# Seven products for the whole second layer from the third block on, with sums and copies that may change engine

## The chip, the core and the metric

The kernel runs on one core of one Trainium2 chip. The metric is the device time of one execution in microseconds. Three runs of the kernel before took 294.63 us (median), 294.39 and 295.84 us. In the profile's rows PE is TensorE (matmuls; PEld its weight loads), DVE is VectorE, ACT ScalarE, POOL GpSimd and SP SyncE.

## The reference, cut to what matters

q, k and v are float32 of 8 batches x 8 heads x 576 positions x 64. Linear attention comes first, then one feed-forward layer over 4608 tokens.

```python
q_s = softmax(q, axis=-1)          # over the 64 of the head
k_s = softmax(k, axis=2)           # over the 576 positions
kv = np.einsum('bhsd,bhse->bhde', k_s, v)
attn = np.einsum('bhsd,bhde->bhse', q_s, kv)
x = attn.transpose(0, 2, 1, 3).reshape(4608, 512)
h = x @ w_in                       # 512 x 2048
g = np.where(h > 0, h, np.exp(np.minimum(h, 0)) - 1)
out = g @ w_out                    # 2048 x 512, float32
```

## The kernel before

Attention works on 16 units (`n`, half of a batch each): q, k and v are loaded, exponentiated on ACT (`stage1`), q is divided by its row sums (reduce and reciprocal on DVE, the product with two SBUF inputs on POOL, a part of the first units on DVE, L441), v is cast to bf16 (L418), q is transposed (`tp` on PE for the first units, later `turn` by DMA and `widen`, a cast, L491/L493), k and v are multiplied (`kv_mm`, L521), scaled (`m`, L530 and L534), and the result is applied to q (`ao_mm`, L552); `xt` copies it (L586, L589) into `XT`, a ring of three blocks.

The feed-forward layer works on nine blocks `j` of 512 tokens. In layer one each block has eight steps `g`; a step is eight 128x128x512 matmuls (`hg_mm`, L637) into a PSUM pair, and steps alternate between two pairs. `hg` then empties the pair: exp on ACT into a buffer `ESB` (L653), a second ACT instruction `relu(1 - e)` in place (L673), and two DVE instructions, here called drains (L676), that combine it with PSUM and write `GR`. PE may use the pair again, two steps later, once the second drain is done. `GR` has 24 units, one and a half blocks.

Layer two of blocks 0 and 1 is plain: `out_mm` (L698) with 512-column matmuls over all 16 tiles of the inner dimension. From block 2 on it uses a seven-product scheme: two token tiles and two halves of the 512 columns form a 2x2 problem, `pair(j, ts)`, two pairs per block, each run while the next block's steps run. The inner dimension is cut into pieces z, two tiles each, gathered in groups.

```python
GROUPS, WHOLE = ((0, 4), (4, 6), (6, 8)), 6
NSP = 6
```

Groups 0 and 1 (12 of 16 tiles) always go by seven products (`mms`, L850, 256-column matmuls). Group 2, the last four tiles, does so only in blocks 6 to 8 (`groups(j)`); in blocks 2 to 5 it goes plainly, by two calls of `std` (L863), four 512-column matmuls each. Each pair and group needs four sums over `GR` (`sums` and `late`, by `add_sum`, L798): S1 = A21 + A22 into `SB`, A21 := A11 - A21, A11 := S1 - A11, A12 := A12 - A11. All are on POOL but those of the very last `late`, which are on DVE. The weights need four combinations per group (`combos`, L769, POOL), once. The products accumulate in PSUM; `copy` (L876, ACT) takes the first, and `dve` (L871) adds the rest into `OSB`, from where SP stores the rows.

The order of every engine's instructions is written out by hand as numbers, `ORDER`, one line of numbers per engine; `Sched.add` records instructions with their dependencies, and `order` and `emit` put them out in that order, with a semaphore wait where a dependency crosses engines. An instruction's engine is fixed in the code. The model times in `Sched` set no waits; they only place some spare matmuls at the start and sort the waits.

Of the kernel before, what the change touches and what calls it, by code (L numbers as in the profile page):

```python
# [21 lines left out]
NSP = 6  # L22
# [78 lines left out]
class Op:  # L101
    __slots__ = ("eng", "dur", "emit", "deps", "key", "idx", "start", "end",
                 "dma", "sem", "val", "clock", "nbytes", "follow", "side", "late", "packet", "margin",
                 "gate", "span", "behind", "early")

    def __init__(self, eng, dur, emit, key, dma=None, nbytes=0):
        self.eng, self.dur, self.emit, self.key = eng, dur, emit, key
        self.deps = {}
        self.dma, self.nbytes = dma, nbytes
        self.start = self.end = None  # L110
        self.behind, self.early = None, 0
        self.follow, self.side, self.packet, self.margin = None, 0, 4608, 0


class Sched:
# [4 lines left out]
    LAND = 350  # L120
    SPIN_FROM, WARM = 5500.0, 11300.0
    FIRST = {"sp": 2050, "act": 2050, "gp": 2700}
    DMA_RATE = 385.0

    def __init__(self, nc):
        self.nc = nc
        self.E = {"sp": nc.sync, "act": nc.scalar, "dve": nc.vector,
                  "pe": nc.tensor, "gp": nc.gpsimd}
        self.ops = []
        self.w = {}  # L130
        self.r = {}
        self.gate = None

    def add(self, eng, dur, emit, key, R=(), W=(), X=(), dma=None, nbytes=0, after=(),
            follow=None, side=0):
        op = Op(eng, dur, emit, key, dma, nbytes)
        op.idx = len(self.ops)
        op.follow, op.side, op.late, op.gate = follow, side, False, self.gate
# [22 lines left out]
    def order(self):  # L161
        line = {e: [self.ops[int(i)] for i in ORDER[e].split()] for e in self.ENG}
        free = {e: 740.0 for e in self.ENG}
        queue = {e: 0.0 for e in self.ENG}
        seq = []
        while any(line.values()):
            before = len(seq)
            for e in self.ENG:
# [104 lines left out]
def t_f32r(n):  # L273
    return (n + 32) / 2.4
# [881 lines left out]
```

## Time and profile before

| | |
|---|---|
| runs | 294.63, 295.84, 294.39 us |
| median | 294.63 us |
| profiled execution, first to last instruction (span) | 292.2 us |
| what the median holds beyond that span | 2.4 us |
| granted TensorE clock | 1.000 over the span |

The page gives no other time of the profiled execution than its span, so what lies around it is taken as the 2.4 us up to the median. A group's row gives the line, the engine, the operation, output <- input with partitions x elements, the count, then after the bar the busy time in us and the mean ns of one, and after the second bar the idle time of the engine just before such instructions, with who ended it. A row of the chain gives start, length and count. A row of waits gives the total in us, how often, and the longest.

### The profile page before, as it was taken

How to read it: one execution, taken by the hardware profiler on the slowest of the kernel's cores; microseconds unless marked ns; L12 is line 12 of the kernel's file. 1: busy time of each engine (PE TensorE's matmuls, PEld its weight loads, DVE VectorE, ACT ScalarE, POOL GpSimd, SP SyncE). 2: the span in 40 equal slices, each digit the busy share in tenths (PEclk: the TensorE clock that was granted, in tenths of full speed). 3: DMA queues.
4: the chain of work that ended last, by engine and by line, in shares of the span. 5: the costliest groups of instructions: out<-in, count | busy, mean ns of one | idle time of the engine just before them, and what ended most of it. 6: DMA issues, size and time to landing. Idle time of an engine off the chain costs nothing.

```text
span 292.2 us, 5351 instructions
## 1 busy us (share of the span) xinstructions
PE 282.1 (97%) x2128; PEld 242.1 (83%) x2128; DVE 177.4 (61%) x326; ACT 211.3 (72%) x249; POOL 220.6 (76%) x216
## 2 busy tenths in 40 slices
PE   2899999999999999999999999999999999999994
PEld 0478887778888888888988888988989889988994
DVE  3748834787464686575656675756542667356753
ACT  4858849988998989786976779856883667665610
POOL 1992435617788999899786979799678968899880
PEclk9999999999999999999999999999999999999999
DMA  7999999799995679577919476403111010400235
GB/s 254 397 367 388 389 389 335 169 281 332 274 316 125 101 232 159 168 182 254 234 45 207 150 157 202 98 16 77 38 36 36 2 31 5 110 0 2 55 90 144
DMA packets 36472, 50.01 MB, mean 171 GB/s; under 512 B 16352, under 2 KB 18144, under 8 KB 36448
## 3 DMA queue, kind: packets, MB, share of 16 engines
q1 hardware_dynamic: 29680, 33.96, 43.5%
q0 software_dynamic: 6528, 15.47, 17.6%
q10 hardware_dynamic: 240, 0.26, 0.4%
q8 instruction: 16, 0.26, 0.4%
q14 instruction: 8, 0.07, 0.1%
HBM read 36.70 MB, written 9.44 MB: 158 GB/s over the span
## 4 chain that ended last, share of the span: by engine, by line
PE 94%; DMA 2%; POOL 2%; SPq 0%; issue 0%; DVE 0%
PE PS L637 46%; PE PS L850 28%; PE PS L698 10%; PE PS L863 5%; PE PS L552 3%; DMA KR<-in_k_dram 2%; PE PS L521 2%; POOL W L379 1%; POOL VB L418 0%; PE PS L465 0%; POOL QS L441 0%; SPq L359 0%; PE PS L564 0%; DVE OSB L871 0%
## 5 line engine op out<-in xcount | busy, mean ns | idle before, releaser
L637 PE MATMUL PS<-XT,W 128*128 128x512 f32 x576 | 142.7, 393 | 0.1
L676 DVE SCALAR_TENSOR_TENSOR GR<-PS,ESB 128x512 fp32r<-128x512 f32 (+1 forms) x124 | 87.5, 705 | 59.6 <-ACT ESB L673 55.7
L637 PEld LDWEIGHTS PS<-XT,W 128*128 128x128 f32 x576 | 105.0, 188 | 21.5 <-DMA W<-in_moe_w_in_dram 0.5
L653 ACT ACTIVATE ESB<-PS 128x1024 f32<-128x1024 f32 x72 | 73.5, 1025 | 38.4 <-PE PS L637 36.9
L673 ACT ACTIVATE ESB<-ESB 128x1024 f32<-128x1024 f32 x64 | 67.8, 1060 | 1.5
L798 POOL TENSOR_TENSOR GR<-GR 128x512 fp32r<-128x512 f32 (+1 forms) x65 | 62.7, 982 | 5.5 <-PE PS L850 4.9
L871 DVE TENSOR_TENSOR OSB<-OSB,PS 128x256 f32<-128x256 f32 x84 | 34.6, 417 | 26.9 <-PE PS L850 25.7
L850 PE MATMUL PS<-W,GR 128*128 128x256 f32 x288 | 45.5, 284 | 0.0
L850 PE MATMUL PS<-TB,GR 128*128 128x256 f32 x288 | 43.8, 283 | 0.0
L441 POOL TENSOR_TENSOR QS<-QR,RZQ 128x1152 f16<-128x1152 f32 (+1 forms) x16 | 30.2, 1886 | 17.2 <-DVE RZQ L433 16.5
L850 PEld LDWEIGHTS PS<-W,GR 128*128 128x128 f32 x288 | 40.8, 190 | 2.0
L850 PEld LDWEIGHTS PS<-TB,GR 128*128 128x128 f32 x288 | 39.9, 191 | 1.7
L798 POOL TENSOR_TENSOR SB<-GR 128x256 fp32r<-128x256 f32 (+1 forms) x31 | 30.0, 973 | 11.4 <-DVE GR L676 10.4
L698 PE MATMUL PS<-W,GR 128*128 128x512 f32 x128 | 32.4, 395 | 0.0
L798 POOL TENSOR_TENSOR GR<-SB,GR 128x256 fp32r<-128x256 f32 (+1 forms) x31 | 29.9, 978 | 2.4 <-PE PS L850 1.9
L418 POOL CAST VB<-VR 128x1152 bf16<-128x1152 f32 (+1 forms) x16 | 17.7, 1106 | 16.1 <-DMA VR<-in_v_dram 16.1
L698 PEld LDWEIGHTS PS<-W,GR 128*128 128x128 f32 x128 | 23.4, 188 | 4.7 <-DVE GR L683 0.2
L430 DVE TENSOR_REDUCE ZQ<-QR 128x18 f32<-128x1152 f32 (+2 forms) x18 | 21.8, 1209 | 6.5 <-ACT QR L428 4.9
L586 ACT ACTIVATE XT<-PS 128x512 fp32r<-128x512 f32 (+6 forms) x32 | 19.2, 603 | 6.8 <-PE PS L552 3.0
L876 ACT ACTIVATE OSB<-PS 128x256 f32<-128x256 f32 x28 | 10.4, 377 | 18.3 <-PE PS L850 9.3
L402 ACT ACTIVATE KR<-KR 128x1152 bf16<-128x1152 f32 x16 | 18.4, 1157 | 0.8 <-DMA KR<-in_k_dram 0.8
L398 ACT ACTIVATE QR<-QR 128x1152 f32<-128x1152 f32 x14 | 16.3, 1161 | 1.5 <-DMA QR<-in_q_dram 1.5
(57 smaller groups left out, 220.4 us busy)
## 6 DMA issues: line engine op xcount, KB each, us to landing
out_dram<-OSB SPq DMA_DIRECT2D x61, 128.0 KB, 2.4
QR<-in_q_dram SPq DMA_DIRECT2D x12, 576.0 KB, 5.0
KR<-in_k_dram SPq DMA_DIRECT2D x12, 576.0 KB, 6.1
VR<-in_v_dram SPq DMA_DIRECT2D x12, 576.0 KB, 5.4
W<-in_moe_w_out_dram POOLq DMA_DIRECT2D x4, 1024.0 KB, 16.6
QR<-in_q_dram POOLq DMA_DIRECT2D x4, 576.0 KB, 12.1
VR<-in_v_dram POOLq DMA_DIRECT2D x4, 576.0 KB, 13.0
KR<-in_k_dram POOLq DMA_DIRECT2D x4, 576.0 KB, 11.1
```

The lines of the kernel that those rows point to most:

```text
L402: S.add("act", t_act(1152, False), lambda e: e.activation(ek[:, :, :, :].rearrange("p h c d -> p (h c d)"), flat(k), AF.Exp), key - 2, X=[ ...
L430: S.add("dve", t_dve(m), lambda e, qp=qp, zp=zp: e.tensor_reduce(zp, qp, AX.X, ALU.add), key - 3, R=[f"qR{i}{x}" for x in xs], W=[f"ZQ{i}{ ...
L441: lambda e, qp=q[:, :, a:b, :], rz=rz, dst=qs[:, :, a:b, :]: e.tensor_tensor(dst, qp, rz, ALU.mult),
L586: S.add("act", t_act((h1 - h0) * n_, True), lambda e, dst=dst, src=src: e.activation(dst, src, AF.Copy), key, W=W, X=X)
L637: last = e.matmul(P[:, t * 512:(t + 1) * 512], self.W1[:, kc, tt * 128:(tt + 1) * 128], self.XT[:, kc, rc:rc + BLK], start=(kc == 0), stop ...
L653: S.add("act", t_act(1024, True), lambda e: e.activation(esb[:, :], self.PS[ps][:, :], AF.Exp), key, W=[f"E{i}"], X=banks)
L673: S.add("act", t_act(1024, False), lambda e: e.activation(esb[:, :], esb[:, :], AF.Relu, bias=1.0, scale=-1.0), key, X=[f"E{i}"])
L676: S.add("dve", t_dve(512 if j else 1024), lambda e, u=u: e.scalar_tensor_tensor(*(x[:, :, u, :] if j else x for x in (gt, P)), 0.0, ev[:, ...
L698: last = e.matmul(dst, self.tile(jb, jj, ts), self.W2[:, jj, c0:c1], start=(jj == 0), stop=(jj == 15))
L798: lambda e: e.tensor_tensor(dst, a, b, op), key, R=R, W=W, X=X, after=after)
L850: last = e.matmul(dst, a[i][:, y_, :], b[i][:, y_, :], start=start and i == 0 and y_ == 0, stop=stop and i == len(grps) - 1 and y_ == z - ...
L871: S.add("dve", t_dve(256), lambda e: e.tensor_tensor(dst, a, b, ALU.add), key, R=R, W=W, X=X, after=after)
```

## The change

- `NSP` becomes 8 and `groups` goes: all three groups go by seven products in every block from 2 on. `std` goes. All `combos` are made at the end of block 2, and group 2's weight combination T1 overwrites the weights' quarter B12 as in the other groups.
- `TB` and `SB` grow to eight pieces. To make room, the two `ESB` buffers lie in `TB` and serve blocks 0 and 1 only. From block 2 on exp is written into the block's own units of `GR` (seen as float32 under the name `GE`), and relu and drains work there in place.
- Copies out of PSUM (`xt`, `tp`, `out_store`, `copy` in `pair`), sums, combinations, casts of v and of the transposed q can each be given to one of two engines. The engine is the one in whose line of `ORDER` the number stands.
- `ORDER` is new for all engines. PE's is the same for its first 34 rows. The constants of the model times are simplified.

In the changed kernel's order 168 sums stand instead of 136, of them 73 on DVE (3 before) and 95 on POOL (133 before). Four of the twelve combinations are on DVE. Four of the 14 later casts of v and seven more of the casts of q are on ACT, and 12 of the copies from PSUM of 256 columns, 3 of 512 and 12 of `xt` on DVE. The diff, cut to its core:

```diff
-NSP = 6
+NSP = 8
 class Sched:
-    def add(self, eng, dur, emit, key, R=(), W=(), X=(), dma=None, nbytes=0, after=(),
-            follow=None, side=0):
+        self.home = {int(i): e for e, line in ORDER.items() for i in line.split()}
+    def add(self, eng, dur, emit, key, R=(), W=(), X=(), dma=None, nbytes=0, after=(), side=0):
+        alts = eng if isinstance(eng, dict) else {}
+        if alts:
+            eng = self.home.get(len(self.ops))
+            eng = eng if eng in alts else next(iter(alts))
+            dur = alts[eng]
...
+        self.GE = nc.alloc_sbuf_tensor_at("GE", [128, 24, 2, 256], F32, offset=nc.sbuf_base - 49152)
-        self.ESB = [a(f"ESB{i}", [128, 1024], F32) for i in range(2)]
-        self.TB2 = nc.alloc_sbuf_tensor_at("TB2", [128, 4, 2, 256], F32R, offset=rbase)
-        self.SB2 = nc.alloc_sbuf_tensor_at("SB2", [128, 2, 128], F32R, offset=rbase + 8192)
+        self.ESB = [at(f"ESB{i}", [128, 1024], F32, offset=tbase + NSP * 1024 + 4096 * i)
+                    for i in range(2)]
...
 def hg(self, j, g, ps, key, how, whole=True):
-        S.add("act", t_act(1024, True), lambda e: e.activation(esb[:, :], self.PS[ps][:, :], AF.Exp), key,
-              W=[f"E{i}"], X=banks)
+        own = gw
+        if j < 2:
+            i = self.eslot % 2
+            self.eslot += 1
+            own = [f"E{i}"]
+            ge = self.ESB[i][:, :].rearrange("p (c u t) -> p c u t", c=2, u=2) if j else self.ESB[i][:, :]
+        S.add("act", t_act(1024, True), lambda e: e.activation(ge, P, AF.Exp), key, W=own, X=banks)
...
 def add_sum(self, grp, dst, a, b, op, key, R, W, X, after):
-        self.S.add(eng, n_ * 2.4 + 60 if eng == "gp" else t_dve(n_),
+        self.S.add({"gp": n_ * 2.4 + 60, "dve": t_dve(n_)}, None,
                    lambda e: e.tensor_tensor(dst, a, b, op), key, R=R, W=W, X=X, after=after)
...
 def pair(self, j, ts, key):
-        grps = self.groups(j)
-        full = 2 in grps
+        grps, tail = (0, 1, 2), j >= WHOLE
...
         def copy(dst, src, W, bk):
-            S.add("act", t_act(256, True), lambda e: e.activation(dst, src, AF.Copy), key, W=W,
+            S.add({"act": t_act(256, True), "dve": t_dve(256)}, None, lambda e: self.copy(e, dst, src), key, W=W,
                   X=[f"b{bk}"])
...
         def second():
-            if not full:
-                std(0, 2 * NSP, 16, False)
+            pass
...
         def fourth():
-            if not full:
-                std(1, 2 * NSP, 16, False)
-            elif not end:
+            if not end:
...
                     if g == 7:
-                        self.combos(key, 0)
-                        self.combos(key, 1)
+                        for grp in range(3):
+                            self.combos(key, grp)
```

More of the change, by code (lines that the diff above doesn't have):

```diff
@@ L102 @@
     __slots__ = ("eng", "dur", "emit", "deps", "key", "idx", "start", "end",
-                 "dma", "sem", "val", "clock", "nbytes", "follow", "side", "late", "packet", "margin",
-                 "gate", "span", "behind", "early")
+                 "dma", "sem", "val", "clock", "nbytes", "side", "early", "alts")
     def __init__(self, eng, dur, emit, key, dma=None, nbytes=0):
@@ L110, in __init__ @@
         self.start = self.end = None
-        self.behind, self.early = None, 0
-        self.follow, self.side, self.packet, self.margin = None, 0, 4608, 0
+        self.side = self.early = 0
 class Sched:
@@ L163, in order @@
         free = {e: 740.0 for e in self.ENG}
-        queue = {e: 0.0 for e in self.ENG}
-        seq = []
+        queue, seq = 0.0, []
         while any(line.values()):
-            before = len(seq)
+            ready = []
             for e in self.ENG:
-                while line[e]:
+                if line[e] and all(d.end is not None for d in line[e][0].deps):
                     o = line[e][0]
-                    near = [d for d in (o.follow, o.gate, o.behind) if d is not None]
-                    if any(d.end is None for d in list(o.deps) + near):
-                        break
-                    t = max([free[e]] + [d.end + self.hop(d, o) for d in o.deps] +
-                            [d.start + (d.dur if d.eng == e else 0) for d in near[:2] if d is not o.behind])
-                    o.start, o.end = t, t + o.dur
-                    free[e] = o.end
-                    if o.dma:
-                        if o.behind is not None:
-                            queue[e] = max(queue[e], o.behind.end - self.LAND - o.behind.margin)
-                        queue[e] = max(t + self.FIRST[e], queue[e]) + o.nbytes / self.DMA_RATE
-                        o.end = queue[e] + self.LAND + o.margin
-                    seq.append(line[e].pop(0))
-            assert len(seq) > before
-        rank = {o: i for i, o in enumerate(seq)}
-        return self.fill(sorted(seq, key=lambda o: (o.start, rank[o])))
+                    ready.append((max([free[e]] + [d.end + self.hop(d, o) for d in o.deps]), e))
+            t, e = min(ready)
+            o = line[e].pop(0)
+            o.start, o.end = t, t + o.dur
+            free[e] = o.end
+            if o.dma:
+                queue = o.end = max(t + self.FIRST[e], queue) + o.nbytes / self.DMA_RATE
+            seq.append(o)
+        return self.fill(seq)
     def hop(self, d, o):
@@ L198, in fill @@
             if o.eng == "pe" and not done:
-                count = int((o.start - free - 20) / 430 if free < self.WARM else
+                count = int((o.start - free - 20) / 421 if free < self.WARM else
                             (o.start - free - 150) / 260)
@@ L412, in stage1 @@
                     dst, src = VB[:, h0:h1, :, 0:D], v[:, h0:h1, :, :]
-                if eng == "act":
-                    S.add("act", t_act(int(576 * (h1 - h0)), False), lambda e, dst=dst, src=src:
-                          e.activation(dst, src, AF.Copy), key - 50, R=[vname], W=[f"VB{vb}{x}"])
-                else:
-                    S.add(eng, 77 + 488 * (h1 - h0) if eng == "gp" else t_dve(int(576 * (h1 - h0))),
-                          lambda e, dst=dst, src=src: e.tensor_copy(dst, src), key - 50,
-                          R=[vname], W=[f"VB{vb}{x}"])
+                cost = {"act": t_act(int(576 * (h1 - h0)), False), "gp": 77 + 488 * (h1 - h0)}
+                S.add(dict(sorted(cost.items(), key=lambda x: x[0] == "act" and vconv != "pair" or x[0] == "gp" and h0 == 5)),
+                      None, lambda e, dst=dst, src=src: self.copy(e, dst, src), key - 50, R=[vname], W=[f"VB{vb}{x}"])
         if "q" not in what:
@@ L436, in stage1 @@
             for a, b, ys in cuts:
-                eng = "gp" if n in self.BYPOOL and ys == [1] or n in self.ALLPOOL else "dve"
                 m = (b - a) * 128
+                cost = {"gp": m * 2.0 + 30, "dve": t_dve(m)}
+                if n in self.BYPOOL and ys == [0]:
+                    cost = {"dve": t_dve(m), "gp": m * 2.0 + 30}
                 rz = self.RZQ[i][:, :, a:b].unsqueeze(3).broadcast_to([128, 2, b - a, D])
-                S.add(eng, m * 2.0 + 30 if eng == "gp" else t_dve(m),
+                S.add(cost, None,
                       lambda e, qp=q[:, :, a:b, :], rz=rz, dst=qs[:, :, a:b, :]: e.tensor_tensor(
@@ L470, in tp @@
             W = [f"qsT{self.alt(n)}{x}" for x in W]
-            if eng == "act":
-                S.add("act", t_act(n_, True), lambda e, dst=dst, src=src: e.activation(
-                    dst, src, AF.Copy), key, W=W, X=X, after=after)
-            else:
-                S.add("dve", t_dve(n_), lambda e, dst=dst, src=src: e.tensor_copy(dst, src),
-                      key, W=W, X=X, after=after)
+            cost = {"act": t_act(n_, True), "dve": t_dve(n_)}
+            S.add(dict(sorted(cost.items(), reverse=eng == "dve")), None,
+                  lambda e, dst=dst, src=src: self.copy(e, dst, src), key, W=W, X=X, after=after)
     def turn(self, n, key):
@@ L489, in widen @@
         src = self.QT[:, :, :].rearrange("p c t -> p (c t)")
-        if n >= LATE:
-            self.S.add("gp", 1080, lambda e: e.tensor_copy(dst, src), key, R=["QT"], W=W)
-        else:
-            self.S.add("act", t_act(1152, False), lambda e: e.activation(dst, src, AF.Copy), key,
-                       R=["QT"], W=W)
+        cost = {"act": t_act(1152, False), "gp": 1080}
+        self.S.add(dict(sorted(cost.items(), reverse=n >= LATE)), None, lambda e: self.copy(e, dst, src), key,
+                   R=["QT"], W=W)
     def side(self, ps, key, *parts):
@@ L758, in combos @@
         z0, z1 = GROUPS[grp]
-        if grp == 2:
-            early = [f"qR0{x}" for x in range(2)] + ["kR0"]
-        else:
-            early = [f"Ox{i}{x}" for i in range(4) for x in "LR"]
-        old, hi = [f"B{grp}"], grp == 2
-        for s, (dst, a, b, W, X, R) in enumerate((
-                (T3, B22, B12, [f"T1{grp}"] + early, [], self.w2(grp)),
-                (T1, B12, B11, [f"T3{grp}"] + [] if hi else [f"T3{grp}"] + self.w2(grp), [], []),
-                (T2, B22, T1, [f"T0{grp}"], [], [f"T3{grp}"]),
-                (T4, B21, T2, [f"T2{grp}"], [], [f"T0{grp}"]))):
-            S.add("gp", (z1 - z0) * 256 * 2.34 + 30, lambda e, dst=dst, a=a, b=b: e.tensor_tensor(
-                dst, a, b, ALU.subtract), key, R=R, W=W, X=X, after=S.ops[-1:] if s == 1 else S.r["qR00"][-1:] if hi and s == 0 else ())
-    def groups(self, j):
-        return (0, 1, 2) if j >= WHOLE else (0, 1)
+        early = [f"Ox{i}{x}" for i in range(z0 // 2, z1 // 2) for x in "LR"]
+        for s, (dst, a, b, W, R) in enumerate((
+                (T3, B22, B12, [f"T1{grp}", f"E{min(grp, 1)}"], self.w2(grp)),
+                (T1, B12, B11, [f"T3{grp}"] + self.w2(grp), []),
+                (T2, B22, T1, [f"T0{grp}"] + early, [f"T3{grp}"]),
+                (T4, B21, T2, [f"T2{grp}"], [f"T0{grp}"]))):
+            n_ = (z1 - z0) * 256
+            S.add({"gp": n_ * 2.34 + 30, "dve": t_dve(n_)}, None, lambda e, dst=dst, a=a, b=b: e.tensor_tensor(
+                dst, a, b, ALU.subtract), key, R=R, W=W, after=S.ops[-1:] if s == 1 else ())
     def sb(self, j, ts, grp):
@@ L805, in sums @@
             S1, N = self.sb(j, ts, grp)
-            own = [f"T1{grp}"] if grp == 2 and (j, ts) != (NBLK - 1, 1) else []
-            one = self.add_sum(grp, S1, A21, A22, ALU.add, key, h + g + own, N, [], self.summed.get(N[0], []))
+            one = self.add_sum(grp, S1, A21, A22, ALU.add, key, h + g, N, [], self.summed.get(N[0], []))
             self.third[j, ts, grp] = self.add_sum(grp, A21, A11, A21, ALU.subtract, key, m, [], h, [one])
@@ L856, in mms @@
                       R=list(names[i]) + ([f"T{wnames}{grp}"] if wnames is not None else self.w2(grp)))
-        def std(p, jj0, jj1, stop):
-            bk = (b0, b1)[p]
-            def mm(e):
-                for jj in range(jj0, jj1):
-                    last = e.matmul(self.bank(bk), self.tile(j, jj, 2 * ts + p), self.W2[:, jj, :],
-                                    start=False, stop=stop and jj == jj1 - 1, skip_group_check=True)
-                return last
-            S.add("pe", (jj1 - jj0) * t_f32r(512), mm, key, side=2, X=[f"b{bk}"],
-                  R=self.gnames(j, ts, range(jj0 // 2, jj1 // 2)) + [
-                      f"W2_{s}" for s in range(jj0 // 4, (jj1 + 3) // 4)])
         def dve(dst, a, b, R, W, X, after=()):
@@ L951, in program @@
         self.xt(1, 0, 0, -10, XT1)
-        for o in S.ops:
-            if o.eng == "pe":
-                o.late = False
         S.spare_after = [self.ident]
```

125 lines of the change are left out of this document (42 added, 83 removed), and 120 rows, old and new, of the table ORDER.

## The prediction

> **What bounds the kernel now.** I read the page's busy times first, then its chain of work that ended last.
>
> ```profile
> span 292.2 us, 5351 instructions
> PE 282.1 (97%) x2128; PEld 242.1 (83%) x2128; DVE 177.4 (61%) x326; ACT 211.3 (72%) x249; POOL 220.6 (76%) x216
> PE 94%; DMA 2%; POOL 2%; SPq 0%; issue 0%; DVE 0%
> ```
>
> PE carries 94% of the chain. The rest lies before 14 us and after the last matmul. Then I looked at the chain in order of time, here one early piece and a stretch in the fourth block:
>
> ```profile
> 54.16 2.14 PE PS L637 x8
> ...
> 102.60 0.93 PE PS L863 x4
> 103.53 1.82 PE PS L637 x8
> 105.35 0.95 PE PS L850 x8
> 106.30 1.84 PE PS L637 x8
> 108.14 1.43 PE PS L850 x12
> ```
>
> From 102 on each piece starts where the one before ends (102.60 + 0.93 = 103.53), so PE waits for nobody: only less PE work shortens the kernel, and only a new wait of PE lengthens it. The rows give my prices: 1.82/8 = 0.2275 us for a 512-column matmul, 0.93/4 = 0.23 for one in L863, 1.43/12 = 0.119 for a 256-column one. The other engines matter only where they release PE. The next rows show how far they are from that, and what their instructions cost.
>
> ```profile
> DVE GR L676 <- ACT ESB L673: 55.7, 46, 5.3
> L653 ACT ACTIVATE ESB<-PS 128x1024 f32<-128x1024 f32 x72 | 73.5, 1025 | 38.4 <-PE PS L637 36.9
> L673 ACT ACTIVATE ESB<-ESB 128x1024 f32<-128x1024 f32 x64 | 67.8, 1060 | 1.5
> L871 DVE TENSOR_TENSOR OSB<-OSB,PS 128x256 f32<-128x256 f32 x84 | 34.6, 417 | 26.9 <-PE PS L850 25.7
> L798 POOL TENSOR_TENSOR GR<-GR 128x512 fp32r<-128x512 f32 x27 | 35.0, 1299 | 4.5 <-PE PS L850 4.3
> L441 POOL TENSOR_TENSOR QS<-QR,RZQ 128x1152 f16<-128x1152 f32 x12 | 25.9, 2155 | 3.5 <-DVE RZQ L433 2.8 <-DMA QT<-QS 0.7
> L418 POOL CAST VB<-VR 128x1152 bf16<-128x1152 f32 x14 | 16.1, 1149 | 16.1 <-DMA VR<-in_v_dram 16.1
> L491 POOL CAST qsT<-QT 128x1152 fp32r<-128x1152 f16 x10 | 11.5, 1154 | 3.4 <-PE PS L552 2.3 <-PE PS L521 1.1
> L769 POOL TENSOR_TENSOR TB<-W 128x1024 fp32r<-128x1024 f32 x2 | 4.8, 2410 | 0.1
> L589 DVE CAST XT<-PS 128x512 fp32r<-128x512 f32 x2 | 1.4, 692 | 2.0 <-PE PS L564 2.0
> L589 DVE CAST XT<-PS 128x256 fp32r<-128x256 f32 x1 | 0.4, 425 | 0.6 <-PE PS L552 0.6
> ```
>
> DVE spends 55.7 us waiting for ACT before its drains (L676): this idle time is PE's cover, because DVE is nearly always ready when a bank is.
>
> **Part one: PE's work.** In blocks 2 to 5 (counted from 0), eight pairs lose two `std` calls of four 512-column matmuls each: 64 of them, 64 x 0.23 = 14.7 us (0.2275 each would give 14.6). Each pair gains seven products of two 256-column matmuls: 8 x 14 = 112, at 0.119 13.3 us. All of it is on the path. Net, with 0.1 for a last group being a little slower after a change of width (1.84 against 1.82 above): **-1.25 us**. [...]
>
> **Part two: who does the rest.** Group 2 adds four sums in each of eight pairs, 32 in all, of 256 elements. The changed order holds 168 sums and 12 weight combinations. On POOL 25 sums of 512 and 13 of 256, 3 combinations of 512 and 1 of 1024, 4 casts of v and 7 of qsT go away:
>
> ```profile
> L798 POOL TENSOR_TENSOR GR<-GR 128x256 fp32r<-128x256 f32 x38 | 28.4, 756 | 1.0 <-PE PS L850 0.6
> ```
>
> 25 x 1.30 + 13 x 0.75 + 3 x 1.30 + 2.4 + 4 x 1.15 + 7 x 1.15 = 61 us, so POOL falls from 221 to 160 us. ACT takes the 11 casts (12.7 us) and gives up 12 copies of 256, 3 of 512 and 12 of XT, some 14 us: no change. DVE takes these copies (16 us, at 0.43, 0.69 and, for XT, the same per column) and 74 more sums and combinations whose two inputs both lie in SBUF (77 against 3): 47 of 256, 29 of 512, one of 1024. Their price is in the last three sums of the old kernel, and in four products of stage one:
>
> ```profile
> L798 DVE TENSOR_TENSOR GR<-GR x3: 417/501/919, 282.4 to 284.1; 128x256 fp32r<-128x256 f32 x2, 128x512 fp32r<-128x512 f32 x1
> L441 DVE TENSOR_TENSOR QS<-QR,RZQ x4: 818/822/974, 8.3 to 37.2; 128x640 f16<-128x640 f32 x4
> 280.79 3.13 POOL L798 TENSOR_TENSOR GR<-GR 128x512 fp32r<-128x512 f32 x3
> 282.40 0.92 DVE L798 TENSOR_TENSOR GR<-GR 128x512 fp32r<-128x512 f32 x1
> 283.70 0.84 DVE L798 TENSOR_TENSOR GR<-GR 128x256 fp32r<-128x256 f32 x2 [0.38 <-PE PS L850]
> 36.47 1.06 POOL L441 TENSOR_TENSOR QS<-QR,RZQ 128x512 f16<-128x512 f32 x1
> 37.24 0.97 DVE L441 TENSOR_TENSOR QS<-QR,RZQ 128x640 f16<-128x640 f32 x1
> ```
>
> The 640-element product takes 0.82 and once 0.97. That one began at 37.24, while POOL's product ran until 36.47 + 1.06 = 37.53; it ended at 38.21, 0.68 after POOL's end. The sum of 282.40 stretched likewise behind POOL's second sum, POOL's three took 3.13 instead of 1.30 + 2 x 0.75 = 2.8, and of the two sums of 256 the one that began before POOL's end took 0.50, the other 0.42. So a sum on DVE that meets a POOL instruction waits out its rest, less about 0.15 that its own start hides (0.29 of rest cost 0.97 - 0.82 = 0.15). Unmet, a sum costs 0.42 (256) or about 0.68 (512, estimate: 0.92 less the 0.24 of its meeting).
>
> DVE's work then is 177 + 16 + 47 x 0.42 + 29 x 0.68 + 1.2 - 1.7 = 232 us (79%), before meetings. POOL is busy with such instructions for some 147 us, half of the span. Weighted by length (65 sums of 0.75, 35 of 1.30, 3 of 2.4, 12 of 2.16, 17 of about 1.15) the rest of one that is met is 0.65 us, 0.5 after the hidden part: **0.25 us for each of the 77 sums, 19 us in all**. Bounds: below, 0.15 a sum, if POOL often idles just then (it waits for DVE's sums, too); above, 0.4, where both run sums back to back. [...]
>
> **Part three: what DVE's lateness does to PE.** Mostly nothing: DVE has 60 us free. But the new order packs sums ahead of drains in one queue, and behind a late sum stand the drains, for which PE's next step on that PSUM pair waits. Take the change from block 6 to 7. Between the last product of block 5 and the product that needs `copy`'s half bank again, PE has two steps (16 x 0.2275) and 38 products' matmuls (38 x 0.119), 8.2 us. A matmul's start lies 0.28 ahead of its end, though the ends are 0.12 apart, and DVE must be done before that start; with 0.2 to 0.3 more on the way at both ends (estimate) about 7.7 is left. DVE has there, in this order, one OSB add, five drains, eight sums (six of 256, two of 512) and the copy.
>
> ```profile
> L850 PE MATMUL PS<-W,GR 128*128 128x256 f32 x288 | 45.5, 284 | 0.0
> L676 DVE SCALAR_TENSOR_TENSOR GR<-PS,ESB 128x512 fp32r<-128x512 f32 x120 | 82.6, 689 | 58.9 <-ACT ESB L673 55.0 <-PE PS L850 2.0
> ```
>
> 0.42 + 5 x 0.69 + 6 x 0.42 + 2 x 0.68 + 0.43 = 8.2, less 0.08 for each of ten that overlap the one before (0.50 + 0.42 took 0.84 above): 7.4. Room 0.3; eight sums at 0.25 cost 2.0; PE waits 1.7. In the same way I count 13.8 us of DVE work in 13.8 with six sums from block 5 to 6 (late by 1.5), and 14.6 in 15.4 with nine, POOL's combinations of 2.4 us beside them, from block 2 to 3 (late by 1.4). Together **+4.6 us**. Each is paid once, since a waiting PE lets DVE catch up. Lighter packings (3 to 4, 4 to 5, in 7) would add up to 1.7; I leave them covered. With 0.15 a sum the three give 2.2, with 0.4 and the lighter ones about 10.
>
> **Smaller edits, at nothing.** `hg` writes exp into GR and works in place, so exp waits for GR's last reader; in the new order those readers end ahead of the step's matmuls, but for the fifth step of blocks 7 and 8 (0.7 us after), whose bank has 5.2 us of PE work against a drain chain of about 4 (1.03 + 1.06 + 2 x 0.69 + hand-overs): covered. Without that cover it is 0.7 each. Start, W1 and W2 loads and first 34 rows of PE are in the same order. SP issues block 0's stores ahead of a transpose and loads; their readers come later. Eleven casts now stand ahead of exps on ACT and could wait for a load:
>
> ```profile
> 66.94 1.15 POOL L418 CAST VB<-VR 128x1152 bf16<-128x1152 f32 x1 [7.22 <-DMA VR<-in_v_dram]
> 81.17 1.15 POOL L418 CAST VB<-VR 128x1152 bf16<-128x1152 f32 x1
> ```
>
> On POOL these waits end at 74 us; the four moved casts of v belong to later blocks. I take 0; bound 7.2. The tail keeps its form.
>
> **The sum.** -1.25 + 4.6 = +3.3: span 295.5. The profiled span lies 2.4 under the runs' median of 294.63, and I keep that distance: **297.9 us**. Its own range, from the bounds of a meeting (2.2 and about 10 in place of 4.6), is 295.6 to 303.
>
> **Rivals.** A: the cover holds. POOL, 61 us lighter, is idle when DVE's sums come, meetings cost under 0.15, and PE runs without gaps: 294.63 - 1.25 = 293.4, 0.4% faster. It decides where the packings' room (0, 0.3, 0.8 us) outlasts six to nine meetings. For it: every other price fits the packing, and a gapless PE before. Against it: the three stretched rows. B: DVE and POOL alternate sum for sum, every meeting costs a whole POOL sum (0.75 to 1.3 less 0.15), some 0.6 a sum, and DVE, 232 + 46 = 278 us, is itself the bound in blocks 2 to 7: late by 8 x 0.6 - 0.3, 3.6 and 4.6 in the three, 12.7, with the lighter ones about 17: 306 to 310. C: a cast on ACT waits for its load and holds exps, up to 7 us: 294 to 301. That the products aren't replaced can't be: the new order has no L863 matmuls.
>
> **Chances.** About 0.5%, 1.5 us, is what a measurement can tell from no change. Forecast 0.53; B 0.05; C 0.03; all slower, 0.61. A and partial cover 0.39: -1.25 is 0.42%, so 0.27 falls within 0.5%, and 0.12 beyond it, where a stray gap of PE (the piece of 54.16 took 2.14 us for eight matmuls, not 1.82) goes too. The range reaches from A with a little more, 293.0, to 303.0, which leaves out about 0.1 on either side.
>
> **What would show it.** Right: sums of 256 on DVE with a mean near 0.6 instead of 0.42; DVE near 250 us, POOL near 165 to 185; PE waits for DVE's drains or copies at the changes of blocks 2-3, 5-6 and 6-7; PE's matmuls alone 1.25 shorter. Wrong: sums at 0.42 with POOL running beside them, or stretched sums and still no gap of PE.

## The result, and the profile after

The changed kernel took 293.75 us (median of 22 runs, 292.96 to 296.69) beside 295.5 us of the kernel before in the same session (22 runs, 294.26 to 297.58). The ratio is 0.9952, 95% interval 0.993 to 0.9973: faster by 0.48%, 1.4 us, at the edge of what can be told from no change. In two later sessions it came out at 0.9964 (0.994 to 0.9989) and 0.9966 (0.9944 to 0.9987). The forecast was 297.9 us, slower. Rival A came true in the main: behind 60 us the cover held. The two profiles differ by less, 292.2 against 291.7 us: the kernel before's is one of its quickest executions (of its 72 in the three later sessions the quickest spans 292.1 us, and the medians lie at 292.6 to 293.5), and what its slower ones lose no profile shows.

First the page of the changed kernel, its span, busy times and chain:

```profile
span 291.7 us, 5471 instructions
PE 281.3 (96%) x2176; PEld 243.8 (84%) x2176; DVE 227.9 (78%) x427; ACT 210.3 (72%) x233; POOL 167.0 (57%) x163
PE 91%; DVE 2%; DMA 2%; POOL 2%; ACT 1%; SPq 0%; issue 0%
```

DVE rose from 177 to 228 us, POOL fell from 221 to 167, and PE is still the bound. Its chain in order of time (start, length, piece), from the point that both kernels reach with the same matmuls behind them to the last matmul, the kernel before first:

```profile
59.06 2.99 PE PS L637 x12
...
273.40 15.15 PE PS L850 x124
```

```profile
59.76 2.11 PE PS L617 x8
...
102.10 1.19 PE PS L803 x10
103.29 1.84 PE PS L617 x8
...
272.56 15.36 PE PS L803 x128
```

From there to the end of the last piece the kernel before needs 273.40 + 15.15 - 59.06 = 229.49 us, the changed one 272.56 + 15.36 - 59.76 = 228.16: 1.33 less, where 1.25 was forecast. Each piece starts where the one before ends. But the changed kernel reaches this point 0.70 later, and its end behind the last matmul is 0.1 longer. PE's waits between 24 and 292 us (total, times, longest) are these two; the kernel before has none:

```profile
PE PS L504 <- POOL VB L274: 0.5, 1, 0.5
PE PS L617 <- DVE GR L656: 0.3, 1, 0.3
```

Both lie before 60 us, far from the three changes of block where the prediction put its waits. Then DVE's sums, by line and shape (busy, mean ns), with the drains (the last column is the idle time ahead of them):

```profile
L754 DVE TENSOR_TENSOR GR<-GR 128x256 fp32r<-128x256 f32 x21 | 10.4, 501 | 0.0
L754 DVE TENSOR_TENSOR GR<-SB,GR 128x256 fp32r<-128x256 f32 x13 | 7.7, 589 | 0.6 <-PE PS L803 0.6
L754 DVE TENSOR_TENSOR SB<-GR 128x256 fp32r<-128x256 f32 x11 | 5.1, 461 | 0.1
L649 DVE SCALAR_TENSOR_TENSOR GR<-PS,GE 128x512 fp32r<-128x512 f32 x112 | 76.9, 688 | 17.2 <-ACT GE L645 15.7
```

A sum of 256 takes 0.46 to 0.59 us on the mean instead of 0.42 unmet: stretched, but by far less than the 0.25 us forecast. The cover of 55 us ahead of the drains has shrunk to 16, and PE did not feel it.

**Which sums meet, and what it costs.** Single rows of DVE and POOL in the changed kernel:

```profile
114.61 2.12 POOL L430 TENSOR_TENSOR QS<-QR,RZQ 128x1152 f16<-128x1152 f32 x1
115.77 1.25 DVE L754 TENSOR_TENSOR GR<-GR 128x256 fp32r<-128x256 f32 x1
...
173.64 1.30 POOL L754 TENSOR_TENSOR GR<-SB,GR 128x512 fp32r<-128x512 f32 x1 [0.24 <-PE PS L803]
173.84 1.38 DVE L754 TENSOR_TENSOR GR<-SB,GR 128x256 fp32r<-128x256 f32 x1 [0.20 <-PE PS L803]
...
204.44 0.75 POOL L754 TENSOR_TENSOR GR<-GR 128x256 fp32r<-128x256 f32 x1
204.68 0.79 DVE L754 TENSOR_TENSOR GR<-SB,GR 128x256 fp32r<-128x256 f32 x1
```

The rests of the POOL instructions were 0.96, 1.10 and 0.51 us, the sums longer than 0.42 by 0.83, 0.96 and 0.37: the rest less 0.13. This holds, within 0.01 us, for the sums that began with more than 0.13 us of a POOL instruction ahead of them; with less, they did not stretch. So the price that the prediction took from two rows (the rest less 0.15) was right. But of the 77 only 20 began beside a running POOL instruction, with 0.42 us of it left on the mean. All the stretching together is 5.9 us, 0.077 for each of the 77. POOL was busy for 61% of the time from 86 to 284 us:

```profile
86.00:284.00 198.00, 198.00 (x1512) 179.31 (x1511) 166.04 (x321) 144.19 (x158) 120.46 (x113) 1.00 0.43 114
```

(POOL is the fifth busy time, 120.46.) Were the two engines independent, 0.61 x 77 = 47 would have met. What keeps them apart is seen at the change from block 6 to 7:

```profile
219.66 1.30 POOL L754 TENSOR_TENSOR GR<-SB,GR 128x512 fp32r<-128x512 f32 x1 [0.21 <-PE PS L803]
...
221.16 1.01 DVE L754 TENSOR_TENSOR SB<-GR 128x256 fp32r<-128x256 f32 x2
222.09 1.02 DVE L754 TENSOR_TENSOR GR<-GR 128x256 fp32r<-128x256 f32 x2
...
223.03 0.42 DVE L754 TENSOR_TENSOR GR<-SB,GR 128x256 fp32r<-128x256 f32 x1
...
223.49 0.42 DVE L754 TENSOR_TENSOR SB<-GR 128x256 fp32r<-128x256 f32 x1
...
223.94 0.42 DVE L754 TENSOR_TENSOR GR<-GR 128x256 fp32r<-128x256 f32 x1
...
224.51 0.75 POOL L754 TENSOR_TENSOR GR<-SB,GR 128x256 fp32r<-128x256 f32 x1 [3.55 <-PE PS L803]
```

Seven of the eight sums that the prediction counted here run while POOL, its own work done at 220.96, waits 3.55 us for a product of PE. None is stretched. The copy behind them ended at 226.53, in time. It is so elsewhere, too: behind each of the 57 sums that met nothing, the next POOL instruction had waited for a sum or combination of DVE (30 times), a drain (11), a reciprocal on DVE (1) or a product of PE (15).

The block works both ways. In the changed kernel 21 POOL instructions began beside one of DVE's sums, and they lasted longer by its rest less 0.14 to 0.15 us, 5.4 us together. A POOL sum of 256 that began at 159.80, for one, took 1.12 us instead of 0.74, since DVE's sum of 512 from 159.64 still had 0.52 to go. So part of the meetings was paid by POOL, which had time to spare.

### The profile page after: what moved, and what is told of

It reads as the page before. It is cut to its first block, busy times and chain, and to the rows that moved or that the text cites. A ratio compares the mean times of both kernels' runs of the same rounds, so it can differ in the third digit from the quotient of the medians.

```text
span 291.7 us, 5471 instructions
## 1 busy us (share of the span) xinstructions
PE 281.3 (96%) x2176; PEld 243.8 (84%) x2176; DVE 227.9 (78%) x427; ACT 210.3 (72%) x233; POOL 167.0 (57%) x163
## 4 chain that ended last, share of the span: by engine, by line
PE 91%; DVE 2%; DMA 2%; POOL 2%; ACT 1%; SPq 0%; issue 0%
PE PS L617 44%; PE PS L803 32%; PE PS L670 10%; PE PS L535 3%; DMA KR<-in_k_dram 2%; PE PS L504 2%; POOL W L374 1%; DVE GR L656 1%; DVE ESB L654 1%; ACT ESB L643 1%; DVE GR L649 0%; POOL VB L274 0%; PE PS L454 0%; POOL QS L430 0%; ACT ESB L645 0%; SPq L356 0%
## 5 line engine op out<-in xcount | busy, mean ns | idle before, releaser
L649 DVE SCALAR_TENSOR_TENSOR GR<-PS,GE 128x512 fp32r<-128x512 f32 x112 | 76.9, 688 | 17.2 <-ACT GE L645 15.7
L643 ACT ACTIVATE GE<-PS 128x1024 f32<-128x1024 f32 x56 | 57.3, 1023 | 43.5 <-PE PS L617 36.9
L754 POOL TENSOR_TENSOR GR<-GR 128x256 fp32r<-128x256 f32 (+1 forms) x51 | 48.1, 960 | 24.0 <-PE PS L803 12.8
L645 ACT ACTIVATE GE<-GE 128x1024 f32<-128x1024 f32 x56 | 59.4, 1061 | 1.5
L803 PE MATMUL PS<-W,GR 128*128 128x256 f32 x336 | 53.5, 283 | 0.0
L803 PE MATMUL PS<-TB,GR 128*128 128x256 f32 x336 | 50.9, 283 | 0.0
L754 POOL TENSOR_TENSOR SB<-GR 128x256 fp32r<-128x256 f32 (+1 forms) x19 | 17.0, 895 | 26.7 <-DVE GR L649 14.6
L754 POOL TENSOR_TENSOR GR<-SB,GR 128x256 fp32r<-128x256 f32 (+1 forms) x21 | 20.9, 1001 | 15.1 <-PE PS L803 11.5
L643 ACT ACTIVATE ESB<-PS 128x1024 f32<-128x1024 f32 x16 | 16.0, 1023 | 5.7 <-PE PS L617 5.1
L754 DVE TENSOR_TENSOR GR<-GR 128x256 fp32r<-128x256 f32 (+1 forms) x33 | 18.7, 577 | 0.6 <-PE PS L803 0.5
```

What stands on the lines that cost most here:

```text
L643: S.add("act", t_act(1024, True), lambda e: e.activation(ge, P, AF.Exp), key, W=own, X=banks)
L645: S.add("act", t_act(1024, False), lambda e: e.activation(ge, ge, AF.Relu, bias=1.0, scale=-1.0), key, X=own)
L649: S.add("dve", t_dve(512 if j else 1024), lambda e, u=u: e.scalar_tensor_tensor(*(x[:, :, u, :] if j else x for x in (gt, P)), 0.0, ge[:, ...
L754: lambda e: e.tensor_tensor(dst, a, b, op), key, R=R, W=W, X=X, after=after)
L803: last = e.matmul(dst, a[i][:, y_, :], b[i][:, y_, :], start=start and i == 0 and y_ == 0, stop=stop and i == len(grps) - 1 and y_ == z - ...
```

## Experiments

Theory 1: the price of a meeting and the packing of the order were as the prediction counted them; the number of meetings was not. Rivals: meetings cost little whatever POOL does, or the room is wide. Four runs test this, two whether the parts pay alone, five where the early 0.8 us goes. All ratios are to the kernel before, run beside them.

**POOL filled.** `FILL` names 29 POOL instructions, with counts, behind which it idled:

```diff
             ins = o.emit(self.E[o.eng])
+            for _ in range(FILL.get(getattr(o, "idx", -1), 0)):
+                self.gen.fill(self.E[o.eng])
...
+    def fill(self, e):
+        if self.fills:
+            e.wait_ge(self.filled, self.fills)
+        self.fills += 1
+        e.tensor_tensor(self.SCR[:, :], self.SCR[:, :], self.SCR[:, :], ALU.add).then_inc(self.filled, 1)
```

> The changed kernel, but where GpSimd idled for 0.9 us or more after 86 us it now adds a scratch tile to itself, 77 instructions of 256 elements and some 0.75 us, so that most of VectorE's sums meet one. It leaves nothing out. Theory 1 (a sum on VectorE waits out the rest of the GpSimd instruction that it meets, less 0.13 us; in the changed kernel only 20 of 77 met one, because GpSimd idles when VectorE sums): 45 or more of 77 are met, stretched by 13 to 20 us in all instead of 6, and PE waits 2 to 6 us: 296 to 300 us. Rival 1 (meetings cost little, whatever GpSimd does): VectorE's sums stay near 0.42 and 0.68 us and the time near 293.7. Rival 2 (they are stretched, but PE's cover is wide): stretched by over 13 us and still no wait of PE, 293.7.

It took 298.11 us, ratio 1.0106 (1.0056 to 1.0155), some 4.2 us more than the changed kernel beside it (0.0142 x 294.7). DVE's largest group of sums (577 ns each in the changed kernel), PE's waits after 60 us, and the place of the longest, first in the changed kernel:

```profile
L763 DVE TENSOR_TENSOR GR<-GR 128x256 fp32r<-128x256 f32 (+1 forms) x33 | 23.3, 715 | 0.3 <-PE PS L818 0.2
```

```profile
PE PS L818 <- DVE OSB L280: 1.5, 1, 1.5
PE PS L626 <- DVE GR L665: 0.4, 1, 0.4
```

```profile
226.18 1.60 PE L803 MATMUL PS<-W,GR 128*128 128x256 f32 x12
```

```profile
226.93 0.87 PE L818 MATMUL PS<-W,GR 128*128 128x256 f32 x6
...
228.88 0.41 DVE L280 COPY OSB<-PS 128x256 f32<-128x256 f32 x1
...
229.34 0.98 PE L818 MATMUL PS<-W,GR 128*128 128x256 f32 x6 [1.54 <-DVE OSB L280]
```

Of the 77 sums 55 began beside a POOL instruction, and the stretching is 15.1 us together, 0.196 for each of the 77, by the same law (two sums apart, where the two instructions began almost together and POOL's waited instead): between the prediction's lower bound and its value. PE then waits for the very copy at the change from 6 to 7 that the prediction named. The view says 1.54 us, but it counts from the end of the row before, and a matmul's row of 256 columns is 0.28 us long while the next one normally begins 0.12 after it. The twelve matmuls that take 1.60 us in the changed kernel reach from 226.93 to 230.32 here, 3.39: 1.79 us are lost (1.7 forecast). Counted in this way, from start to start of the same matmuls, this execution loses 3.6 us behind 60 us against the changed kernel's profile, some of it in waits too short for the view.

Both rivals are out: meetings do cost, and the cover is not wide. With meetings nearer to the number that I had assumed, the time comes near the forecast. That 298.11 and 297.9 agree so closely is partly luck: the stretch was 0.196 a sum and not 0.25, and PE lost 3.6 us in the profile and not 4.6. The profiled execution, 296.54 us, was the quickest of four; what the other three, up to 2.4 us slower, lost beyond it is open.

**Lateness without meetings.**

```diff
-                   lambda e: e.tensor_tensor(dst, a, b, op), key, R=R, W=W, X=X, after=after)
+                   lambda e: [self.late_by(e), e.tensor_tensor(dst, a, b, op)][-1], key, R=R, W=W, X=X, after=after)
...
+    def late_by(self, e):
+        if e is self.nc.vector:
+            i = self.lates = getattr(self, 'lates', -1) + 1
+            e.tensor_reduce(self.SCQ[:, i % 40:i % 40 + 1], self.SCR[:, 0:LATE_BY], AX.X, ALU.add)
```

> The changed kernel, but ahead of each of the 77 sums and combinations on VectorE stands a dummy sum along one row of a scratch tile, some 0.25 us long: the lateness that the prediction gave each sum for meeting GpSimd, without a meeting. It leaves nothing out. Theory 1 (the prediction's count of the room at the changes of blocks 2-3, 5-6 and 6-7 was right, only the meetings were too many): PE waits there, at least 4.6 us in all, 298 us or more. Rival (the room is larger than counted and the lateness would have been hidden): PE stays gapless, under 294.5 us.

It took 303.84 us, ratio 1.0292 (1.0251 to 1.0333), 9.7 us over the changed kernel. (The dummy stands ahead of the 73 sums; the four combinations have none.) PE's longest waits after 60 us:

```profile
PE PS L811 <- DVE OSB L275: 1.7, 1, 1.7
PE PS L619 <- DVE GR L651: 1.6, 4, 0.9
PE PS L537 <- DVE XT L275: 1.1, 1, 1.1
```

A dummy delays its sum by 0.246 us (median from start to start). The later sums met POOL more often, too, 26 times, and stretched by 11.1 us: 0.25 + 0.14 = 0.39 us a sum in all. The prediction gave about 10 for 0.4 a sum with the lighter packings. Start to start, PE loses 10.7 us behind 62 us in this profile (304.41 us, the slowest of four): 3.0 at the change from 6 to 7, 1.5 from 5 to 6, 2.9 from 2 to 3, and 3.3 elsewhere. By the prediction's rooms 0.39 a sum makes 2.8, 2.3 and 2.7 of these, and up to 1.7 elsewhere. The rival is out.

> As the run with a dummy sum ahead of each of VectorE's 77 sums, with 80 elements instead of 176, some 0.13 us each. Theory 1 (the room is as the prediction counted it: 0.3, 0 and 0.8 us at three changes, and little more elsewhere): PE waits 1.5 to 4 us, 296 to 298. Rival (there is a threshold between 0.08, which the changed kernel bears on the mean, and 0.25 us): under 0.7 us of new waits, 294.5 or less.

With 80 elements a dummy delays by 0.146 us, 0.22 with the meetings. 295.91 us, ratio 1.0022 (0.9999 to 1.0045), some 1.8 us more than the changed kernel's 0.996 in three sessions. After 60 us PE waits 0.6 for the same copy and 0.2 elsewhere; 1.2 in place of 0.5 lie at 58 us, at a load. Start to start, PE loses 2.5 us behind 62 us. By the prediction's rooms it should be nearly 4 for 0.22 a sum. So the room at a small lateness is larger than I counted. One packing by itself shows by how much:

> The changed kernel with the dummy sum of 176 elements, 0.25 us, ahead of eight sums alone: the eight that VectorE runs between 221 and 226 us at the change from block 6 to 7, none of which met a GpSimd instruction in the changed kernel. Theory 1 (the room there is 0.3 us, as the prediction counted, or up to 0.8, as the run with GpSimd filled suggests): PE waits 1.2 to 1.7 us for the copy that frees its half bank, the kernel is 1.2 to 1.7 us slower than the changed kernel. Rival (the order behind absorbs it): no wait of PE there over 0.3 us.

```diff
+LATE_ONES = (1052, 1075, 1053, 1076, 1066, 1077, 1078, 1131)
```

295.43 us, ratio 1.0009 (0.9988 to 1.003), beside 0.9966 of the changed kernel in the same session: 1.3 us slower. PE waits once after 60 us, between the same twelve matmuls:

```profile
226.02 0.88 PE L812 MATMUL PS<-W,GR 128*128 128x256 f32 x6
...
228.42 0.98 PE L812 MATMUL PS<-W,GR 128*128 128x256 f32 x6 [1.53 <-DVE OSB L276]
```

They reach from 226.02 to 229.40, 3.38 us instead of 1.60: 1.78 are lost. Eight dummies are 2.0 us, and two of the sums, now late, met POOL for 0.36 more. 2.33 of lateness cost 1.78: the room is 0.55 us, not 0.3. With POOL filled the same eight sums were stretched by 2.36 and PE lost 1.79, the same room again. In the changed kernel the copy ends 0.37 us ahead of its product's matmul (226.53 against 226.90, the seventh of the twelve), and 0.06 of that is needed (228.36 to 228.42 here), so 0.3 is the copy's own; the rest is DVE's idle time on the way (0.20 ahead of the drain at 224.57, for ACT), which lateness fills first.

**The parts alone.** First the products without the moved sums: 76 numbers go from DVE's line of `ORDER` to POOL's.

> The changed kernel with 76 of VectorE's 77 sums and combinations back on GpSimd, each put into its queue at the time at which VectorE would start it; the seven products for the whole width stay. It leaves nothing out. GpSimd's work is then some 167 + 46 x 0.75 + 29 x 1.3 + 2.4 = 241 us. Theory 1 (the sums had to move for the products to pay: GpSimd at 83% runs late against PE's need): PE waits for GpSimd's sums, over 2 us, 296 us or more. Rival (GpSimd keeps up, as in the kernel before with 221 us): PE gapless, 293.5 to 294.

312.54 us, ratio 1.0615 (1.0574 to 1.0655). PE's waits after 60 us:

```profile
PE PS L803 <- POOL SB L754: 7.0, 6, 3.8
PE PS L803 <- POOL GR L754: 3.3, 8, 1.3
```

The sums had to move for the products to pay, in this order at least. Then the moved sums without the products, in the kernel before:

```diff
+        eng = "dve" if len(self.S.ops) in DVE_SUMS else eng
         self.S.add(eng, n_ * 2.4 + 60 if eng == "gp" else t_dve(n_),
```

> The kernel before with one part of the change alone: the 61 sums that it shares with VectorE's 77 of the changed kernel run on VectorE, each put into its queue at the time at which GpSimd would start it; products, other work and other orders stay. It leaves nothing out. Theory 1 (a sum on VectorE costs PE nothing by itself; VectorE had 60 us free): 294.7, ratio 1.00, PE gapless, GpSimd near 160 us. Rival (the place in the queue decides, and an order that wasn't made for it meets and holds drains): PE waits over 1.5 us, 296.5 or more.

296.9 us, ratio 1.0079 (1.0047 to 1.0111): 2.3 us slower, the rival's side. Of its 64 sums on DVE 23 began beside a POOL instruction and the stretching is 8.1 us together, 0.13 for each of the 64 against 0.077. Its waits view shows only 0.7 us for PE after 60 us, but start to start the same 2128 matmuls lose 2.7 us against the kernel before's profile: 0.7 near 235 us, 0.6 between 240 and 260, 0.7 between 110 and 170, and the rest in smaller pieces. For most of these pieces the view names no releaser. Its order puts the sums where the old one had them on POOL; the changed kernel's was made for them.

**The early 0.8 us.**

> The changed kernel once more, beside the others on one chip. Theory 1 (the change saves 1.25 us of matmuls and loses about 0.7 us of it before 60 us, where block 0's stores now stand ahead of a load of v): 0.995 of the kernel before, and the profile shows the matmuls of the keys and values waiting about 0.5 us for the cast of v near 58 us again. Rival (that gap was a chance of one execution): no such wait this time.

294.02 us, ratio 0.9964 (0.994 to 0.9989). The waits came again: 0.43 us at 59.1 and 0.27 at 60.8. (This execution has one more, 1.10 us near 16 us for a load of weights, which the first one lacks.) The place in the kernel before, then in the changed one:

```profile
55.41 1.15 POOL L418 CAST VB<-VR 128x1152 bf16<-128x1152 f32 x1 [1.87 <-DMA VR<-in_v_dram]
...
57.05 0.69 DVE L681 TENSOR_SCALAR ESB<-ESB 128x1024 f32<-128x1024 f32 x1 [1.09 <-ACT ESB L653]
```

```profile
46.33 4.57 SPq L699 DMA_DIRECT2D out_dram<-OSBX  x5
...
56.76 1.15 POOL L274 CAST VB<-VR 128x1152 bf16<-128x1152 f32 x1 [3.38 <-DMA VR<-in_v_dram]
56.94 1.51 DVE L654 TENSOR_SCALAR ESB<-ESB 128x1024 f32<-128x1024 f32 x1 [1.09 <-ACT ESB L643]
...
58.05 0.78 PE L504 MATMUL PS<-VB,KR 64*64 64x65 bf16 x72 [0.51 <-POOL VB L274]
```

The cast of v begins 1.35 us later. Its load was issued by POOL, at 50.49 us (50.67 in the kernel before), and landed at 56.70 (55.36): it was in flight with the five stores that SP now issues from 46.33 to 50.9. PE waits for the cast, and the clipping L654 of a drain now meets the cast (rest 0.97 us) and lasts 1.51 instead of 0.69 us. I tried to undo it by moving the stores (184 190 189 180 181) in SP's line, first right behind the transpose and the load of q:

```diff
-        "8 9 10 11 12 13 184 190 189 180 181 204 206 209 219 228 187 218 235 229 301 183 238 302 "
+        "8 9 10 11 12 13 204 206 184 190 189 180 181 209 219 228 187 218 235 229 301 183 238 302 "
```

> The changed kernel with one edit: SyncE issues five stores of block 0 behind the transpose and the load of q, as the kernel before does, not ahead of them. Theory 1: the load of v lands about 1.3 us earlier (cast near 55.4 instead of 56.8 us), PE is gapless from 14 us on as in the kernel before, the span falls by 0.5 to 0.8 us: 293.0 beside 293.7 of the changed kernel. Rival (the gap comes from the other new orders or is chance): no change, 293.7, and the wait stays.

A miss: 295.02 us, ratio 0.9999 (0.9976 to 1.0023). The early waits are gone, but a load of v behind the stores is issued at 58.73 instead of 57.93 us, and a cast that stands on ACT since the change waits for the transpose behind them, until 70.03 instead of 68.26 (what rival C feared):

```profile
70.03 1.16 ACT L274 ACTIVATE qsT<-QT 128x1152 fp32r<-128x1152 f16 x1 [2.31 <-DMA QT<-QS]
...
71.24 0.62 PE L535 MATMUL PS<-qsT,MBLK 128*128 128x384 f32 x2 [1.60 <-ACT qsT L274]
```

Then behind the loads of 64 us:

```diff
+        "8 9 10 11 12 13 204 206 209 219 228 187 218 235 229 184 190 189 180 181 301 183 238 302 "
```

> The changed kernel with one edit: SyncE issues the five early stores of block 0 behind the loads that it issues near 64 us, ahead of the third transpose, where its queue is empty and the DMA engines fall idle near 70 us. Theory 1 (in the changed kernel these stores hold up one load of v for the cast near 57 us, and put back right behind the first transpose they held up the next load and the second transpose instead): no wait of PE from 14 to 290 us, 0.8 us less than the changed kernel, 293.1. Rival (the loads after 64 us are as tight, and the third transpose or a cast of q waits instead): a wait of 0.5 to 2 us between 64 and 80 us, 294 to 295.

293.09 us, ratio 0.9951 (0.9921 to 0.9981), six of its twelve runs under 293.1 and six over. The loads were in time, but in the profiled execution POOL's product, released earlier, now stands beside the clipping:

```profile
56.42 2.12 POOL L430 TENSOR_TENSOR QS<-QR,RZQ 128x1152 f16<-128x1152 f32 x1
...
57.22 1.88 DVE L654 TENSOR_SCALAR ESB<-ESB 128x1024 f32<-128x1024 f32 x1 [1.09 <-ACT ESB L643]
...
60.41 2.12 PE L617 MATMUL PS<-XT,W 128*128 128x512 f32 x8 [1.18 <-DVE GR L656]
```

Rest 56.42 + 2.12 - 57.22 = 1.32, less 0.13 is 1.19, and 0.69 + 1.19 = 1.88: the law to the hundredth. So POOL was made to wait:

```diff
+            self.S.ops[227].deps[self.S.ops[255]] = "raw"
             self.S.emit(self.S.order())
```

> The changed kernel with the five early stores of block 0 issued behind the loads near 64 us, as in the run before, and with a wait more: the product of GpSimd that began at 56.42 us there (the scaled q of the third batch) waits for VectorE's clipping beside it (ESB in place, near 57.2 us). Theory 1 (that clipping lasted 1.88 us instead of 0.69 because it waited out the rest of this product, and PE's 1.2 us of waiting came from it): the clipping takes 0.69 us, PE is gapless from 24 to 288 us, 0.8 us less than the changed kernel on the same chip, about 0.992 of the kernel before. Rival (the load of v or the transpose behind the product is late next): a new wait of 0.5 us or more between 57 and 75 us, no faster than the changed kernel.

```profile
57.24 0.69 DVE L655 TENSOR_SCALAR ESB<-ESB 128x1024 f32<-128x1024 f32 x1 [1.09 <-ACT ESB L644]
...
58.02 2.12 POOL L431 TENSOR_TENSOR QS<-QR,RZQ 128x1152 f16<-128x1152 f32 x1 [1.80 <-DVE ESB L655]
```

292.9 us (292.73 to 293.67, six runs), ratio 0.9927 (0.9899 to 0.9955), and PE waits for nothing between 24 and 292 us. So the clipping was the cause of that wait, and the rival is out. The changed kernel beside it:

> The changed kernel once more, on the chip of the two runs beside it, as their measure: 0.995 to 0.997 of the kernel before, with waits of PE of 0.7 us in all between 47 and 62 us.

294.22 us (293.46 to 295.02, twelve runs), ratio 0.9966 (0.9944 to 0.9987). The early waits came a third time, 0.41 and 0.27 us, with two more that the first two profiles of the changed kernel lack, 0.34 near 66 and 0.33 near 156 us. The medians of the two versions lie 1.3 us apart, of which the early waits are half; the intervals of their ratios overlap, so between these two only the direction is likely. Against the kernel before the version with the wait is 0.7% faster.

## Why the prediction was wrong

**Part one was right:** 1.33 us less matmul work, 1.25 forecast.

**Part two's price was right, its count failed; this is the step that turned the sign.** "The rest of one that is met" less 0.15 measured as the rest less 0.13. But I let a sum meet POOL with the share of the span in which POOL is busy, half, as if the two ran independently. They don't: POOL's sums wait for PE's products and for DVE's drains and sums, so POOL is idle while DVE works off what it waits for (42 of the 57 unmet sums; PE's products account for the other 15). 20 of 77 met instead of half, with 0.42 us left instead of 0.65: 0.077 a sum and 5.9 us in all, for 0.25 and 19. My lower bound, 0.15, still lay twice too high, though its reason, that POOL waits for DVE's sums, was the true one.

**Part three's places were right, its rooms a little small.** The copy at 6 to 7 is the tightest place, as the runs with dummies show; its room is 0.55 us, not 0.3. The 0.3 was what the copy itself had to spare; DVE's 0.2 of idle time on the way was left out. The 0.2 to 0.3 "on the way at both ends" was an estimate of mine; the rows show 0.06 from the copy to its matmul (228.36 to 228.42) and, in the changed kernel, 0.04 from a product's end to DVE's add (218.46 + 0.40 to 218.90). The +4.6 follows from 0.25 a sum; with no stretch among the eight there, it is 0. Around the other two changes PE lost 1.5 and 2.9 us with the 0.39 us a sum of the longer dummies, near the 2.3 and 2.7 of the prediction's rooms, and 0.4 and 0.1 with 0.22, where they give 1.3 and 1.2. (The prediction's 2.2 for 0.15 a sum is 2.35 by its own rooms, 0.9 + 0.9 + 0.55; it changes nothing.)

**One smaller edit was not free.** The stores moved ahead on SP were taken at nothing with "their readers come later". The readers did, but a load of v that was in flight with them is needed earlier: 0.7 to 0.8 us, more than half of what the products gain.

**Totals.** POOL at 167 us fits (165 to 185 forecast; 160 without meetings, and 5.4 of the rest are its own waits for DVE's sums). DVE at 228 does not (250): the meetings are 13 us fewer, and the sum of 232 adds whole rows, while instructions behind one another overlap by 18 us in the changed kernel (246.2 added up, 227.9 busy) and by 8 in the kernel before (185.0 and 177.4). Rival A gave 293.4 and named its condition, meetings under 0.15, which is what happened; B and C did not come, C only in an order of my own. The chance of 0.39 for A and partial cover looks too low, for a reason that was at hand: A had named the mechanism, POOL idle when DVE's sums come; I weighed it against three stretched rows, which show the price of a meeting and nothing of how often one comes, and did not follow through the new order which product or drain each POOL sum waits for.

## What to carry to other kernels

When two engines block each other, don't multiply one's busy share by the other's count; look at what each waits for: work that waits for the other engine did not meet it here (20 of 77 met, where the busy share gave 47). Price a meeting from single rows, then count the meetings place by place in the order. Where an order is tight, the place of each piece counts: the moved sums without an order made for them cost 2 us here, and put back on the other engine 18. Stores moved ahead in one queue were paid here by a load issued from another (landed at 56.70 instead of 55.36 us), and mending one wait showed the next, so take a new trace after each mend. Short waits hide between pipelined instructions (0.7 us of PE's waits in the view, 2.7 from start to start, with the sums moved alone): compare the starts of the same instructions in two profiles before calling a difference open.

## What the runs showed of the hardware

The block between DVE and POOL follows one rule in these rows, rest less 0.13 us, for sums with two SBUF inputs, and within 0.02 us for the clipping with one (1.51 and 1.88 us instead of 0.69, with rests of 0.97 and 1.32). A POOL instruction that comes second waits likewise, rest less 0.14 to 0.15. The dummy reductions, with one input, did not last longer beside a busy POOL: 23 of the 73 began beside a POOL instruction and took 0.32 to 0.34 us (all, min, median and max in ns):

```profile
L762 DVE TENSOR_REDUCE SCQ<-SCR x73: 279/327/340, 89.7 to 293.7; 128x1 f32<-128x176 f32 x73
```

Where PE waited 3.8 us at one time (the longest wait of the run with the sums on POOL), its next matmuls ran at a granted clock of 0.50:

```profile
106.00:110.00 4.00, 2.00 (x9) 2.00 (x10) 1.38 (x2) 1.14 (x3) 3.92 (x6) 0.67 0.66 255
110.00:114.00 4.00, 4.00 (x13) 3.23 (x12) 0.00 (x0) 0.74 (x2) 2.65 (x3) 0.50 0.00 0
```

The third number from the end is the granted clock, 0.67 and 0.50; eight matmuls at 110.50 took 3.41 us, the eight at 115.29 took 1.84. So 1.57 us came on top of the wait here; around the waits of 1.5 us of two other runs the granted clock stayed at 1.00. This is one place in one execution, and no run here shows what set the clock.
